# Smaller steps, earlier loads, another order of the second sweep, and the sums of w1 on VectorE, in a fused retention and mixture-of-experts kernel

## The chip, the cores and the metric

The kernel runs on one core of one Trainium2 chip. The metric is device time in microseconds (us), taken as the median of several executions. Engines are named as the profile names them: PE is TensorE (PEld its weight loads), DVE is VectorE, ACT is ScalarE, POOL is GpSimd, SP is SyncE, which here only issues DMAs.

## The reference

```python
def _attn_ref(q, k, v):                       # B, H, S, D = 4, 8, 768, 64
    gamma = 1.0 - 2.0 ** (-5.0 - np.arange(H))
    for t in range(S):
        state = gamma[None, :, None, None] * state + einsum('bhd,bhe->bhde', k[:, :, t], v[:, :, t])
        y[:, :, t] = einsum('bhd,bhde->bhe', q[:, :, t], state) / sqrt(D)

def _moe_ref(x, w_gate, w1, w2):              # N, D, E, F = 3072, 512, 8, 1024
    logits = x @ w_gate
    P = np.exp(logits - logits.max())
    for _ in range(8):
        P /= P.sum(1, keepdims=True) + 1e-09
        P /= P.sum(0, keepdims=True) + 1e-09
        P *= N / E
    for e in range(E):
        out += P[:, e:e + 1] * (np.maximum(x @ w1[e], 0.0) @ w2[e])
```

The output of the first function, laid out as 3072 tokens by 512, is the x of the second.

## The kernel before

The program has three stages, and within each engine the instructions run in the order in which the code is written: no scheduler moves them, and every queue, SP's DMA queue too, is served in order.

**Attention.** The retention is computed in 24 chunks of 128 steps (6 chunks for each of 4 batch entries). The loop variable is `tau`. One pass loads the four raw tiles of chunk tau + 3 (`loads`), splits q and k of chunk tau + 2 into a rounded part and a remainder (`split_qk`: `kh`, `QH` on ACT, `QL` on DVE, `kl` on POOL), computes the scores of chunk tau + 1 (`ps_s`, then `ta` on DVE), the gate logits of chunk tau - 1, and the result of chunk tau (`attend`: `ps_x`, `RX`), which SP stores to `xd`; `state` updates the running state with `tk` and `st` from POOL. Four chunks make a position c of the sequence. After pass `tau == 2 * B` (8) the loop also works off a list `todo`, two tasks a pass, which prepares the next stage.

**First product** (x @ w1, relu). It is a Strassen-like scheme: each 2x2 block product is made with seven products M1 to M7 of sums of blocks. For x these sums and their split into rounded part (hi, ACT) and remainder (lo) are made by `x_tasks`, from tiles that `x_load` fetches from `xd`; XSC holds the sums for a while. There are three groups r of two sequence positions; X0 holds r = 0 and later r = 2, X1 holds r = 1. For w1 one job is one 512 KB load into one half of RW (`w1_load`), four sums of 128x256 (`adds`), the rounding of the 7 blocks and two remainders (3 and 4 blocks) into one of three buffers WA (`w1_tasks`).

`UnitA` is one output block: seven products of 6 matmuls of 128x512, each followed by work on its PSUM bank. A row of the main loop (variable n, 96 rows) walks through `ROW`, seven places m = 0 to 6: M6 of unit n, M1 of unit n + 1, M3, M7, M2 of n + 1, M5 of n + 1, M4. The DVE work of a row is, by the profile's lines, L213 and L214 (after M3), L218 (after M7), L225 (after M2), L234 and L236 (`sums`, m = 4) and L240 (`last_sum`, m = 0 of the next row). Four PSUM banks are shared: M5 reuses M3's bank, M4 reuses M7's, so PE can go on only when DVE has read them.

The first 32 rows (the first sweep) run r = 0 with a new w1 job in each row; a job is prepared in the row two ahead of its use, from the queue `wq` at places m = 0, 1 and 5. The queue `xq` prepares X1 in rows 0 to 10 and, from row 32 on, the tile X0 for r = 2. Then the second sweep runs r = 1 and r = 2: units 29, 30, 31 with r = 1, the same three with r = 2, and then each unit with both. `order` is the list that says which job, unit and r a row has. A list `sink` holds the Sinkhorn steps (max, exp, eight times `sink_a` and `sink_b`, a transpose), one per row from row 12 on; each uses DVE and small matmuls at the end of a row.

**Second product** (h @ w2, weighted sum): the third stage reads the stored h back; the change doesn't touch its code.

Of the kernel before, what the change touches and what calls it, by code (L numbers as in the profile page):

```python
# [47 lines left out]
def kernel(  # L48
# [60 lines left out]
    def x_load(t, r):  # L109
        for i, c, d in ((M1, 0, 0), (M7, 1, 0), (M3, 1, 1), (M2, 0, 1)):  # L110
            for k in range(2):
                sp.dma_start(rd(t[:, XP[i], 1, k * 512:(k + 1) * 512]).rearrange("p (b s) -> p b s", s=C),  # L112
                             xd[2 * r + c][:, :, 2 * d + k, :])

    def x_tasks(t, engs):
        q = []
        sc = {M7: 0, M5: 1, M6: 2, M4: 3}
        e = [engs[k % len(engs)] for k in range(22)]
        for k in range(2):
# [6 lines left out]
            def tt(o, a, b, src=src):  # L126
                eng = e.pop()
                q.append(lambda: eng.tensor_tensor(XSC[:, sc[o], :], a, b, ALU.subtract))

            def one(i, w=w, src=src):  # L130
                eng = e.pop()

                def f():
                    hi_act(w(i, 0), src(i))
                    lo(eng, w(i, 1), src(i), w(i, 0))
                q.append(f)

            b12 = rd(w(M7))
            tt(M5, b12, src(M1))
            tt(M6, src(M3), src(M5))  # L140
            tt(M7, src(M3), b12)
            tt(M4, src(M2), src(M6))
            for i in (M1, M5, M2, M6, M7, M3, M4):
                one(i)
# [677 lines left out]
```

## Time and profile before

| what | value |
|---|---|
| median of 3 runs | 2055.17 us (2054.22 to 2057.34) |
| the profiled execution, its own time | 2053.89 us |
| its span | 2051.8 us |
| mean granted TensorE clock | 0.987 |
| busy PE / DVE / ACT / POOL | 1985.9 / 1527.7 / 1041.7 / 406.0 us |
| HBM read and written | 269.31 and 232.88 MB |
| first matmul of the first product | at 166.28 us |
| first row of the second sweep, loads of X0 issued | at 501.27 us |

A line of a timeline gives start, duration, engine, line of the code, operation, tile written and tiles read, shape, count of instructions merged, and in brackets how long the engine stood idle before and what it waited for. A line of a table by stretches gives, for each engine, its busy time and the number of instructions begun; PEclk is the granted clock as a share of full speed.

### The profile page before, as it was taken

The numbers are of one execution on the slowest core, as the hardware profiler recorded it, in microseconds if no ns is written. First come the engines' busy times: TensorE is split into PE (matmuls) and PEld (weight loads), VectorE is DVE, ScalarE is ACT, GpSimd is POOL, SyncE is SP. The second block draws the span as 40 slices with busy tenths as digits, with TensorE's granted clock in tenths as the row PEclk, the third lists the DMA queues.
The fourth block names the chain that finished last, engine by engine and source line by source line (L and its number), as shares of the span: only waits on it lengthen the run. The fifth ranks groups of instructions, "written<-read, shape, count | busy, mean of one in ns | idle before, by whom it ended". The sixth has DMA issues, their size and how long they took to land.

```text
span 2051.8 us, 28824 instructions
## 1 busy us (share of the span) xinstructions
PE 1985.9 (97%) x9273; PEld 1647.2 (80%) x9273; DVE 1527.7 (74%) x2083; ACT 1041.7 (51%) x1668; POOL 406.0 (20%) x422
## 2 busy tenths in 40 slices
PE   7797999998899999999999999999999999999998
PEld 7786887887688888888887788888888888888887
DVE  6795988995666666666677787878778777868766
ACT  3343564554444444444444565655555555655553
POOL 5462342341211121121123000100100101001001
PEclk9899999999999999999999999999999999999999
DMA  7755776776466666666667888998999999999997
GB/s 240 239 180 163 242 245 206 244 244 217 165 233 214 218 228 217 221 218 223 220 229 263 297 286 281 278 288 277 285 283 278 267 291 270 291 292 269 271 269 184
DMA packets 253191, 504.13 MB, mean 246 GB/s; under 512 B 27824, under 2 KB 40432, under 8 KB 250992
## 3 DMA queue, kind: packets, MB, share of 16 engines
q1 hardware_dynamic: 241088, 458.78, 66.3%
q0 software_dynamic: 11952, 43.52, 11.0%
q8 instruction: 72, 1.18, 0.2%
q14 instruction: 79, 0.65, 0.1%
HBM read 269.31 MB, written 232.88 MB: 245 GB/s over the span
## 4 chain that ended last, share of the span: by engine, by line
PE 90%; DVE 4%; DMA 3%; issue 1%; ACT 1%; SPq 1%; POOL 0%; DVEq 0%; ACTq 0%
PE psA L190 42%; PE psA L551 25%; PE psB L551 19%; DMA raw<-kT 1%; DVE QL L80 1%; PE ps_s L327 1%; PE ps_x L363 1%; DMA RW<-w 1%; PE psA L372 1%; PE ps_x L358 0%; PE ps_t L339 0%; DVE X L80 0%; DVE ta L330 0%; SPq L112 0%; DMA hd<-OT 0%
## 5 line engine op out<-in xcount | busy, mean ns | idle before, releaser
L190 PE MATMUL psA<-X,WA 128*128 128x512 f32 x4032 | 931.4, 393 | 24.1 <-DVE OT L213 18.8
L190 PEld LDWEIGHTS psA<-X,WA 128*128 128x128 f32 x4032 | 760.8, 189 | 190.2 <-DVE OT L213 20.9
L77 ACT ACTIVATE WA<-WA 128x512 fp32r<-128x512 f32 x668 | 403.1, 629 | 259.3 <-PE psB L551 116.7
L551 PE MATMUL psA<-WA,X 128*128 128x512 f32 x2296 | 531.4, 389 | 0.2 <-DVE XSC L562 0.2
L551 PEld LDWEIGHTS psA<-WA,X 128*128 128x128 f32 x2296 | 431.0, 188 | 89.9 <-issue 0.6
L551 PE MATMUL psB<-WA,X 128*128 128x512 f32 x1728 | 404.3, 390 | 5.1 <-ACT WA L77 3.1
L80 DVE TENSOR_TENSOR WA<-WA,WA 128x512 fp32r<-128x512 f32 x487 | 313.7, 685 | 99.4 <-ACT WA L77 94.9
L551 PEld LDWEIGHTS psB<-WA,X 128*128 128x128 f32 x1728 | 324.6, 188 | 74.8 <-ACT WA L77 4.2
L158 POOL TENSOR_TENSOR RW<-RW 128x256 f32<-128x256 f32 x244 | 220.8, 915 | 637.9 <-DMA RW<-w 412.8
L219 ACT ACTIVATE OT<-OT 128x512 f32<-128x512 f32 x96 | 60.7, 632 | 243.3 <-DVE OT L218 243.3
L80 DVE TENSOR_TENSOR WA<-RW,WA 128x768 fp32r<-128x768 f32 x122 | 142.5, 1169 | 54.0 <-ACT WA L77 53.9
L569 POOL DMA_DIRECT2D out<-XSC x56 | 48.5, 865 | 611.7 <-DVE XSC L564 365.6
L80 DVE TENSOR_TENSOR WA<-WA 128x512 fp32r<-128x512 f32 x181 | 121.7, 697 | 35.4 <-ACT WA L77 34.4
L213 DVE TENSOR_TENSOR OT<-psA,OT 128x512 f32<-128x512 f32 x96 | 66.2, 689 | 106.2 <-PE psA L190 106.2
L77 ACT ACTIVATE WA<-RW 128x768 fp32r<-128x768 f32 x122 | 109.4, 946 | 23.6 <-POOL RW L158 13.9
L225 DVE TENSOR_TENSOR OT<-psA,OT 128x512 f32<-128x512 f32 x96 | 66.2, 690 | 58.5 <-ACT OT L219 51.3
L229 ACT ACTIVATE OT<-psA 128x512 f32<-128x512 f32 x96 | 57.5, 599 | 77.1 <-PE psA L190 40.3
L236 DVE TENSOR_TENSOR OT<-OT 128x512 f32<-128x512 f32 x96 | 92.2, 961 | 3.3
L579 ACT ACTIVATE OT<-psA 128x512 f32<-128x512 f32 x96 | 57.4, 598 | 72.7 <-PE psA L551 68.8
L226 ACT ACTIVATE OT<-OT 128x512 f32<-128x512 f32 x96 | 60.7, 633 | 65.4 <-DVE OT L225 65.3
L240 DVE TENSOR_TENSOR OT<-OT 128x512 f32<-128x512 f32 x96 | 70.1, 730 | 30.0 <-ACT OT L229 26.1
L211 ACT ACTIVATE OT<-psA 128x512 f32<-128x512 f32 x96 | 57.4, 598 | 64.0 <-PE psA L190 63.9
(116 smaller groups left out, 1486.4 us busy)
## 6 DMA issues: line engine op xcount, KB each, us to landing
hd<-OT SPq DMA_DIRECT2D x672, 256.0 KB, 2.6
WA<-hd SPq DMA_DIRECT2D x668, 256.0 KB, 6.1
RW<-w SPq DMA_DIRECT2D x61, 512.0 KB, 4.5
out<-XSC POOLq DMA_DIRECT2D x56, 512.0 KB, 8.3
RW<-w SPq DMA_DIRECT2D x16, 1024.0 KB, 7.7
out<-OT POOLq DMA_DIRECT2D x27, 512.0 KB, 8.4
OT<-pd SPq DMA_DIRECT2D x23, 512.0 KB, 6.2
raw<-kT SPq DMA_DIRECT2D x24, 256.0 KB, 4.0
```

The source lines that it names most:

```text
L77: act.activation(o, i, AF.Copy)
L80: eng.tensor_tensor(o, full, rd(h), ALU.subtract)
L158: eng_add.tensor_tensor(x[:, WP[o]], x[:, WP[p]], x[:, WP[q]], op)
L190: pe.matmul(ps, w[:, a, k * P:(k + 1) * P], x[:, b, k * 512:(k + 1) * 512], start=i in PRE and k == 0 and m == 0, stop=k == 1 and m == 2, ...
L213: dve.tensor_tensor(c12, ps, u2, ALU.add)
L219: act.activation(o, o, AF.Relu)
L225: dve.tensor_tensor(o, ps, s1, ALU.add)
L226: act.activation(o, o, AF.Relu)
L229: act.activation(self.new("A12"), ps, AF.Relu)
L236: dve.tensor_tensor(t["S2"], t["S1"], t["A11"], ALU.subtract)
L240: dve.tensor_tensor(self.new("S4"), self.t["A12"], self.t["S2"], ALU.subtract)
L551: pe.matmul(ps[d] if isinstance(ps, tuple) else ps[:, d, :], w[:, a, q * 256 + d * P:q * 256 + d * P + P], h[b], start=i in PRE and q == 0 ...
```

## The change

It has six parts.

- The loads of X0 for r = 0 are split: the first position after pass 5, the second after pass 8, there behind the two w1 loads. The task list then starts with the two w1 jobs (POOL sums, now in a step of their own; the rounding is a second step), followed by the x tasks; it is run from pass 10 on. Two more w1 loads are issued after pass 16 instead of at the first rows.
- `x_tasks` becomes 22 equal steps: one subtraction (always DVE) or one remainder, and at most one rounding on ACT for a later step.
- In the rows, `w1_tasks` has four steps at m = 0, 3, 5 and 6, and its sums run on DVE instead of POOL.
- X1 is prepared from row 1 on, two steps a row; X0 for r = 2 from row 33 on, five steps a row, two remainders in seven on POOL.
- The second sweep runs units 29 to 31 with r = 1, units 28, 27, 26 with r = 1 and then r = 2, units 29 to 31 with r = 2 (their w1 is loaded and prepared a second time, so there are 64 jobs instead of 61), and then as before.
- The max becomes three sink steps and the exp three of six operations; the list starts at row 14, and the transpose comes at row 38.

```diff
-    def x_load(t, r):
-        for i, c, d in ((M1, 0, 0), (M7, 1, 0), (M3, 1, 1), (M2, 0, 1)):
-            for k in range(2):
+    def x_load(t, r, which=(0, 1)):
+        for i, c, d in ((M1, 0, 0), (M2, 0, 1), (M7, 1, 0), (M3, 1, 1)):
+            for k in range(2) if c in which else ():
...
+            def step(n, w=w, src=src):
+                b12 = rd(w(M7))
+                hi = [M1, M2, M5, M6, M7, M3, M4][n] if n < 7 else None
+                if n < 4:
+                    o, a, b = [(M5, b12, src(M1)), (M6, src(M3), src(M5)), (M7, src(M3), b12), (M4, src(M2), src(M6))][n]
+                    dve.tensor_tensor(XSC[:, sc[o], :], a, b, ALU.subtract)
+                else:
+                    i = [M1, M5, M2, M6, M7, M3, M4][n - 4]
+                    lo(engs[n % len(engs)], w(i, 1), src(i), w(i, 0))
+                if hi is not None:
+                    hi_act(w(hi, 0), src(hi))
...
+        def rounded():
             hi_act(a[:, 0:3, 0, :], x[:, 0:3, :])
             hi_act(a[:, 3:7, 0, :], x[:, 3:7, :])
...
-        return [adds, lambda: rest(slice(0, 3)), lambda: rest(slice(3, 7))]
+        return [adds, rounded, lambda: rest(slice(0, 3)), lambda: rest(slice(3, 7))]
...
-    for g in [[NJ - 3, NJ - 2, NJ - 1]] + [[j] for j in range(NJ - 4, 2, -1)] + [[2, 1, 0]]:
-        order += [(j if j >= NJ - 3 else 2 * NJ - 4 - j, j, r) for r in (1, 2) for j in g]
+    order += [(j, j, 1) for j in (NJ - 3, NJ - 2, NJ - 1)]
+    order += [(NJ + k, NJ - 4 - k, r) for r in (1, 2) for k in range(3)]
+    order += [(NJ + 3 + k, NJ - 3 + k, 2) for k in range(3)]
+    for g in [[j] for j in range(NJ - 7, 2, -1)] + [[2, 1, 0]]:
+        order += [(2 * NJ - 1 - j, j, r) for r in (1, 2) for j in g]
...
+                if tau == B + 1:
+                    x_load(X0, 0, (0,))
                 if tau == 2 * B:
-                    x_load(X0, 0)
                     w1_load(0)
                     w1_load(1)
-                    todo += x_tasks(X0, [dve]) + w1_tasks(0, pool, dve) + w1_tasks(1, pool, dve)
-                if tau > 2 * B:
+                    todo += [f for g in zip(w1_tasks(0, pool, dve), w1_tasks(1, pool, dve)) for f in g]
+                    x_load(X0, 0, (1,))
+                    todo += x_tasks(X0, [dve])
+                if tau > 2 * B + 1:
                     run(todo, 2)
+                if tau == 4 * B:
+                    w1_load(2)
+                    w1_load(3)
...
-        sink = [sink_max, sink_exp] + [sink_a, sink_b] * SINKHORN + [sink_t]
+        sop = sink_exp()
+        sink = [sink_max, sink_max2, sink_max3]
+        sink += [lambda k=k: run(sop, 6) for k in range(3)]
+        sink += [sink_a, sink_b] * SINKHORN + [sink_t]
...
-                wq += w1_tasks(conv, pool, dve)
+                wq += w1_tasks(conv, dve, dve)
...
-                xq = x_tasks(X0, [dve, pool])
+            if n == NJ + 1:
+                xq = x_tasks(X0, [dve, dve, pool])
...
-                if m in (0, 1, 5):
+                if m in (0, 3, 5, 6):
                     run(wq, 1)
-                if m in (1, 6) or n >= NJ:
-                    run(xq, 2 if n >= NJ else 1)
+                if m in (1, 6) or n >= NJ and m in (0, 3, 5):
+                    run(xq, 1)
```

How this stands on the engines is shown at three places. First DVE, in a row of the first sweep in which X1 is prepared: of the row's names, X is X1, OT holds temporary and output blocks, psA the PSUM banks. Before:

```order
L80 TENSOR_TENSOR WA_72<-RW,WA_72 128x3x256
L80 TENSOR_TENSOR X_1773<-XSC,X_1773 128x512
L213 TENSOR_TENSOR OT<-psA_256,OT 128x512
L214 SCALAR_TENSOR_TENSOR OT<-OT 128x512
L218 TENSOR_TENSOR OT<-psA_253,OT 128x512
L225 TENSOR_TENSOR OT<-psA_255,OT 128x512
L234 SCALAR_TENSOR_TENSOR OT<-OT 128x512
L236 TENSOR_TENSOR OT<-OT 128x512
L80 TENSOR_TENSOR WA_72<-RW,WA_72 128x4x256
L80 TENSOR_TENSOR X_1773<-X_1773 128x512
L240 TENSOR_TENSOR OT<-OT 128x512
```

And now, on the same engine, in such a row:

```order
L152 TENSOR_TENSOR RW<-RW 128x256 x4
L80 TENSOR_TENSOR X_1775<-X_1775 128x512
L209 TENSOR_TENSOR OT<-psA_256,OT 128x512
L210 SCALAR_TENSOR_TENSOR OT<-OT 128x512
L214 TENSOR_TENSOR OT<-psA_253,OT 128x512
L221 TENSOR_TENSOR OT<-psA_255,OT 128x512
L230 SCALAR_TENSOR_TENSOR OT<-OT 128x512
L232 TENSOR_TENSOR OT<-OT 128x512
L80 TENSOR_TENSOR WA_71<-RW,WA_71 128x3x256
L80 TENSOR_TENSOR WA_71<-RW,WA_71 128x4x256
L80 TENSOR_TENSOR X_1775<-XSC,X_1775 128x512
L236 TENSOR_TENSOR OT<-OT 128x512
```

The four sums stand ahead of the reads of PSUM (now L209 to L221), and both remainders of w1 stand together behind the row's sums.

Second, DVE in row 35, the third row of the second sweep in which X0 is prepared for r = 2 (L131 and L80 on X_70), with w1 job 34:

```order
L152 TENSOR_TENSOR RW<-RW 128x256 x4
L80 TENSOR_TENSOR X_70<-XSC,X_70 128x512
L131 TENSOR_TENSOR XSC<-X_70 128x512
L209 TENSOR_TENSOR OT<-psA_256,OT 128x512
L210 SCALAR_TENSOR_TENSOR OT<-OT 128x512
L214 TENSOR_TENSOR OT<-psA_254,OT 128x512
L131 TENSOR_TENSOR XSC<-X_70,XSC 128x512
L221 TENSOR_TENSOR OT<-psA_255,OT 128x512
L230 SCALAR_TENSOR_TENSOR OT<-OT 128x512
L232 TENSOR_TENSOR OT<-OT 128x512
L80 TENSOR_TENSOR WA_72<-RW,WA_72 128x3x256
L131 TENSOR_TENSOR XSC<-X_70 128x512
```

Before, the same preparation stood in rows 32 and 33, fourteen tasks a row, with every second operation on POOL.

Third, SP around pass 8 of the attention, where the raw tiles of chunk 12 (raw0 to raw3) are loaded. Before:

```order
L368 DMA xd2_77<-RX_280 128x512
L112 DMA X0_70<-xd0_75 128x4x128 x2
L112 DMA X0_70<-xd1_76 128x4x128 x4
L112 DMA X0_70<-xd0_75 128x4x128 x2
L152 DMA RW_73<-w1 128x1024 x2
L284 DMA raw0_887<-qT 128x512
L284 DMA raw1_889<-kT 128x512
```

And now:

```order
L367 DMA xd2_77<-RX_280 128x512
L146 DMA RW_73<-w1 128x1024 x2
L112 DMA X0_70<-xd1_76 128x4x128 x4
L283 DMA raw0_887<-qT 128x512
L283 DMA raw1_889<-kT 128x512
```

Four of the eight loads of X0 left this place; they stand in the same way ahead of the raw tiles of chunk 9.

More of the change, by code (lines that the diff above doesn't have):

```diff
@@ L124, in src @@
                 return XSC[:, sc[i], :] if i in sc else rd(w(i))
[L126 to L144, printed above, removed]
+            def step(n, w=w, src=src):
[9 more added lines that the diff above has]
+                    hi_act(w(hi, 0), src(hi))
+            q += [lambda n=n, step=step: step(n) for n in range(11)]
         return q
@@ L459, in sink_exp @@
             dve.tensor_copy(mx, ps[:, 0:1])
+        def sink_exp():
             x, n, r, q = [et[:, i, :] for i in range(4)]
             s1, s2 = [ei[:, i, :].bitcast(mybir.dt.int32) for i in range(2)]
-            l2 = L.rearrange("p a b -> p (a b)")
-            dve.tensor_scalar(x, l2, mx, -104.0, ALU.subtract, ALU.max)
-            dve.tensor_scalar(n, x, LOG2E, MAGIC, ALU.mult, ALU.add)
-            dve.tensor_scalar(n, n, MAGIC, None, ALU.subtract)
-            dve.scalar_tensor_tensor(r, n, -LN2_HI, x, ALU.mult, ALU.add)
@@ L467, in sink_exp @@
-            dve.scalar_tensor_tensor(r, n, -LN2_LO, r, ALU.mult, ALU.add)
-            dve.tensor_scalar(x, n, -126.0, None, ALU.max)
-            dve.tensor_tensor(n, n, x, ALU.subtract)
-            dve.tensor_scalar(s1, x, 127.0, 8388608.0, ALU.add, ALU.mult)
-            dve.tensor_scalar(s2, n, 127.0, 8388608.0, ALU.add, ALU.mult)
-            dve.tensor_scalar(q, r, EXPC[0], None, ALU.mult)
-            for c in EXPC[1:]:
-                dve.scalar_tensor_tensor(q, q, c, r, ALU.add, ALU.mult)
@@ L475, in sink_exp @@
-            p2 = Pm.rearrange("p a b -> p (a b)")
-            dve.scalar_tensor_tensor(q, q, 1.0, s1.bitcast(F32), ALU.add, ALU.mult)
-            dve.tensor_tensor(p2, q, s2.bitcast(F32), ALU.mult)
+            l2, p2 = [t.rearrange("p a b -> p (a b)") for t in (L, Pm)]
+            ops = [
+                lambda: dve.tensor_scalar(x, l2, mx, -104.0, ALU.subtract, ALU.max),
+                lambda: dve.tensor_scalar(n, x, LOG2E, MAGIC, ALU.mult, ALU.add),
+                lambda: dve.tensor_scalar(n, n, MAGIC, None, ALU.subtract),
+                lambda: dve.scalar_tensor_tensor(r, n, -LN2_HI, x, ALU.mult, ALU.add),
+                lambda: dve.scalar_tensor_tensor(r, n, -LN2_LO, r, ALU.mult, ALU.add),
+                lambda: dve.tensor_scalar(x, n, -126.0, None, ALU.max),
+                lambda: dve.tensor_tensor(n, n, x, ALU.subtract),
+                lambda: dve.tensor_scalar(s1, x, 127.0, 8388608.0, ALU.add, ALU.mult),
+                lambda: dve.tensor_scalar(s2, n, 127.0, 8388608.0, ALU.add, ALU.mult),
+                lambda: dve.tensor_scalar(q, r, EXPC[0], None, ALU.mult),
+            ]
@@ L479, in sink_a @@
+            ops += [lambda c=c: dve.scalar_tensor_tensor(q, q, c, r, ALU.add, ALU.mult) for c in EXPC[1:]]
+            ops += [
+                lambda: dve.scalar_tensor_tensor(q, q, 1.0, s1.bitcast(F32), ALU.add, ALU.mult),
+                lambda: dve.tensor_tensor(p2, q, s2.bitcast(F32), ALU.mult),
+            ]
+            return ops
         def sink_a():
@@ L714 @@
             UA[0].post(i)
-        loaded = 3
+        loaded = 4
         PS2 = None
@@ L760 @@
                 loaded += 1
-            if 12 <= n < 12 + len(sink):
-                sink[n - 12]()
+            if 14 <= n < 13 + len(sink):
+                sink[n - 14]()
+            if n == 38:
+                sink[-1]()
         carry.last_sum()
```

10 lines of the change are left out of this document (5 added, 5 removed).

## The prediction

> **What bounds the kernel now.** I read the page's busy times first, then the chain of work that ended last, then TensorE's matmuls by stretches, and last the timelines at the places where the stretches lose time. The busy times and one piece of the chain (start, length, what):
>
> ```profile
> PE 1985.9 (97%) x9273; PEld 1647.2 (80%) x9273; DVE 1527.7 (74%) x2083; ACT 1041.7 (51%) x1668; POOL 406.0 (20%) x422
> 537.53 571.94 PE psA L190 x2520
> 505.25 5.66 DMA X<-xd
> 171.86 6.85 DMA RW<-w
> ```
>
> TensorE bounds it. In the undisturbed piece a matmul takes 571.94 / 2520 = 0.227 us, so a row of the first product (42 matmuls) takes 9.53 us, and nothing of the change makes a matmul shorter: it can only win or lose time in which TensorE waits. The matmuls of line L190 alone, by stretches (length, PE busy and count, PEld, granted clock, DMA share, GB/s), show where it does:
>
> ```profile
> 166.20:202.20 36.00, 28.06 (x108) 22.10 (x108) 0.91 0.61 188
> 202.20:307.70 105.50, 105.01 (x457) 84.93 (x456) 1.00 0.74 244
> 307.70:341.00 33.30, 27.96 (x108) 22.19 (x109) 0.90 0.61 192
> 341.00:500.00 159.00, 159.00 (x692) 128.89 (x691) 1.00 0.70 233
> 500.00:540.00 40.00, 27.56 (x102) 20.68 (x101) 0.87 0.53 170
> 540.00:1109.00 569.00, 569.00 (x2510) 470.50 (x2509) 1.00 0.64 221
> ```
>
> Length minus count times 0.227 is the loss: 11.5 us at the start, 1.8 in the rows that prepare X1, 8.8 at the max and the exp, 1.9 in the Sinkhorn rows (mostly the small matmuls, which stay), 16.8 where X0 is prepared for r = 2, none after. That is 40.8 us, all that can be won here. The rest, attention, ends at 166 us.
>
> **The start, 11.5 us.** The chain shows w1 job 2 landing late: its load is issued at 171.86, behind the loads of X1, and takes 6.85 us; job 3 follows in the same way. The change issues both after pass 16, more than 30 us earlier, and X1's steps begin one row later. I leave 1.0: gain 10.5.
>
> **The rows with the sums on DVE.** This is the part that can turn against it, since every row's PSUM reads stand behind the sums on an engine that is nearly full. One row of DVE while POOL was idle, the remainder of three blocks, and the prices near a sum of 128x256:
>
> ```profile
> 182.23 0.68 DVE L213 TENSOR_TENSOR OT<-psA,OT 128x512 f32<-128x512 f32 x1
> ...
> 184.50 0.69 DVE L225 TENSOR_TENSOR OT<-psA,OT 128x512 f32<-128x512 f32 x1 [0.26 <-ACT OT L207]
> ...
> 186.43 1.22 DVE L80 TENSOR_TENSOR WA<-RW,WA 128x1024 fp32r<-128x1024 f32 x1
> 187.57 0.68 DVE L128 TENSOR_TENSOR XSC<-X,XSC 128x512 f32<-128x512 f32 x1
> 188.17 0.69 DVE L240 TENSOR_TENSOR OT<-OT 128x512 f32<-128x512 f32 x1
> ...
> 397.60 0.95 DVE L80 TENSOR_TENSOR WA<-RW,WA 128x768 fp32r<-128x768 f32 x1
> 398.47 0.68 DVE L213 TENSOR_TENSOR OT<-psA,OT 128x512 f32<-128x512 f32 x1
> L661 DVE TENSOR_TENSOR RW<-RW 128x512 f32<-128x512 f32 x56 | 38.3, 684 | 0.0
> L483 DVE TENSOR_TENSOR Pm<-Pm,rs 128x192 f32<-128x192 f32 x7 | 2.5, 358 | 0.2
> L158 POOL TENSOR_TENSOR RW<-RW 128x256 f32<-128x256 f32 x244 | 220.8, 915 | 637.9 <-DMA RW<-w 412.8
> L80 DVE TENSOR_TENSOR WA<-RW,WA 128x1024 fp32r<-128x1024 f32 x61 | 82.7, 1357 | 0.0
> L236 DVE TENSOR_TENSOR OT<-OT 128x512 f32<-128x512 f32 x96 | 92.2, 961 | 3.3
> ```
>
> From start to start: L213 to L225 less its wait 2.01, L225 to the remainder of four blocks 1.93, that remainder 1.14, L240 as long as the step at L128, 0.60, the remainder of three blocks 0.87: 6.55 us. A sum isn't in the trace; its bounds are 0.36 (128x192) and 0.68 (128x512), and between them by the count of elements 0.42, nearest to the smaller one. Four of them make 1.7, the row 8.25, against 9.53 of TensorE. Two steps of X1 add 1.2: 9.45, just under. So rows 1 to 11 cost nothing, as long as POOL leaves DVE alone, and it does: the same remainder that took 1.22 alone has a mean of 1.36, and L236 one of 0.96 against 0.69, because POOL's sums run beside them, and these are gone. I leave 1.5 of the 1.8 lost now: gain 0.3.
>
> **The sink.** Its rows, and the stall that the exp makes:
>
> ```profile
> 323.16 1.93 DVE L474 SCALAR_TENSOR_TENSOR XSC<-XSC 128x192 f32<-128x192 f32 x5
> 329.98 15.38 PE L190 MATMUL psA<-X,WA 128*128 128x512 f32 x54 [2.88 <-DVE OT L213]
> 385.68 0.15 DVE L489 TENSOR_SCALAR ct<-pcs 128x8 f32<-128x8 f32 x1
> 386.38 0.68 DVE L240 TENSOR_TENSOR OT<-OT 128x512 f32<-128x512 f32 x1
> 395.24 0.34 DVE L480 TENSOR_REDUCE rs<-Pm 128x24 f32<-128x192 f32 x1
> 397.00 0.68 DVE L240 TENSOR_TENSOR OT<-OT 128x512 f32<-128x512 f32 x1
> ```
>
> `sink_a` takes 1.76 and `sink_b` 0.70. With the sums a row with `sink_a` needs 10.0 (0.5 over), the next 8.95 (0.6 under); DVE may lag some 1.5 us before TensorE stands, since M5 needs M3's bank only two products later, but what it makes good in the second row it can only make good while it lags. Between nothing and 0.5 for each of the 7 `sink_a` before row 33: I take 2.0. Three rows with six operations of the exp at 0.39 or less need up to 10.6: 2.0. The small matmuls stay, 1.9. So 5.9 instead of 10.7, and the transpose no longer waits for a max in its own row: gain 4.8.
>
> **The second sweep.** The stall of 16.8 us begins with the loads of X0 for r = 2 (in the chain above), which can't start before row 31 is done, and the fourteen tasks a row behind them. Now r = 2 is wanted in row 37, five rows later, so the loads are covered by rows 32 to 34, and 22 steps are spread over rows 33 to 37. What is late next is DVE: rows 33, 34 and 35 each carry a w1 job (8.25), three to five steps at 0.60 on DVE, and a sink step: 11.95, 11.8 and 11.95. That is 7.1 over, less the 1.5 of lag: 5.6 (nothing to 10). Jobs 29 to 31 done again add 3 x 3.7 on DVE in rows 39 to 41, which have 8.25 and no other work, and 1.5 MB of loads at a DMA share of 0.64: hidden. Gain 11.2.
>
> **Attention, about nothing.** The eight loads of X0 and two of w1 after pass 8 hold up the raw tiles of chunk 12 and all behind (SP, ACT, PE, and two stretches of all engines: PE, PEld, DVE, ACT, POOL, clock):
>
> ```profile
> 63.70 6.97 SPq L112 DMA_DIRECT2D X<-xd  x8
> 72.44 0.65 SPq L284 DMA_DIRECT2D raw<-kT  x1
> 79.54 0.63 ACT L77 ACTIVATE kh<-raw 128x512 fp32r<-128x512 f32 x1 [14.61 <-DMA raw<-kT]
> 84.37 0.55 PE L327 MATMUL ps_s<-QH,kh 128*128 128x256 f32 x1 [10.28 <-DVE ta L330]
> 78.00:84.00 6.00, 0.00 (x0) 0.00 (x0) 3.22 (x3) 2.92 (x5) 3.75 (x3) 0.50 0.85 325
> 84.00:90.00 6.00, 5.63 (x26) 5.66 (x27) 5.89 (x11) 1.78 (x3) 1.65 (x2) 0.50 0.60 179
> 149.03 1.06 ACT L77 ACTIVATE WA<-RW 128x1024 fp32r<-128x1024 f32 x1 [3.46 <-POOL RW L158]
> ```
>
> TensorE stands 10.3 us and then runs a while at half its clock, some 4 us more. Four of the loads (3.5 us of issue) now stand in front of chunk 9 instead: a stall there of about 3.5, and one of about 5.5 after pass 8, with the half clock behind at least the second, 4. That is 13 to 17 against 14.3. The eight POOL sums (8 x 0.915 = 7.3 us) now stand in one block after pass 10, ahead of `tk`, `kl` and `st` of the next pass; TensorE waits for the raw tiles just then, which hides them; without that cover they cost up to 7. In exchange ACT no longer stands 3.46 us behind POOL near the end, and the remainders no longer wait for their rounding. The two w1 loads after pass 16 cost about 1. I take 0, between -8 and +10.
>
> [...]
>
> **Sum.** 10.5 + 0.3 + 4.8 + 11.2 + 0 = 26.8 us. The profiled execution took 2053.89 (its span 2051.8 and 2.1 around it), 1.3 under the median of the runs. 2053.9 - 26.8 = 2027; by the median 2028. I say 2029, for small waits of the first rows that I haven't priced.
>
> **Rivals.**
>
> (a) DVE can't carry the rows; slower. If a sum costs 0.80, midway between DVE's row of 512 and POOL's 0.915 for the same sum, a row is 9.75: over by 1.4 in the 11 rows with X1, by 1.45 on average in the 13 rows of `sink_a` and `sink_b`, by 2.5 in the three of the exp, by 0.2 in the 5 others, and rows 33 to 35 lose 4.6 more: 47.5 us, where the sum above has 5.5. That is 42 more, 2071. For it speaks that all of PSUM's sums wait on this one engine; against it the 0.36 for 192 elements. It ends above the kernel before from 0.72 a sum on; at 0.5 it gives 2035. 7 in 100.
>
> (b) The sums wait for their load on DVE. POOL waited for it 412.8 us in all, at no cost; DVE would stand with every PSUM read behind it. A half of RW is free only when the remainder at the end of row n is done, and the sums come at the start of row n + 2, nearly 10 us later, against some 5 for issue and landing. If 0.5 us a row is lost on 30 rows: 2044. 9 in 100.
>
> (c) Attention pays: both stalls run into the half clock and POOL's block isn't covered: 10 more, 2039. 17 in 100.
>
> (d) Attention gains: the split loads mostly hide in the slack, and the shorter tail counts: 8 less, 2021. 16 in 100.
>
> **How the numbers follow.** The forecast, 2029 with its own range of 2024 to 2035, has 50 in 100. The range takes in (d) and (b) with what lies around them and leaves out (a) at the top: 2018 to 2047. Within 0.2% (2051 to 2059, about what a measurement of this kernel can tell from no change) lie only mixtures, several terms at their bad ends, 9 in 100; slower is (a), 7; faster 84.
>
> **What would show it.** Right: L190 begins near 166 us; the stretches at the start and at the exp lose under 2 and under 4 us; POOL has nothing between attention and the end of the first product but four steps on X0; the sums at L152 take 0.40 to 0.45, and TensorE's waits lie in rows 33 to 36. It would be wrong if matmuls wait for L209 in most rows of the first sweep (a), if L152 waits for RW (b), or if L190 begins over 8 us from 166 (c, d).

## The result and the profile after

| kernel | median (us) | runs | ratio to the kernel before, 95% interval |
|---|---|---|---|
| before | 2055.16 (2054.22 to 2057.34) | 4 | |
| changed | 2034.4 (2030.9 to 2036.94) | 4 | 0.9896 [0.9881, 0.9912] |
| changed, run again | 2033.05 (2027.32 to 2036.51) | 6 | 0.9904 [0.9886, 0.9922] |

The change makes the kernel 1.0% faster. The time lies in the range (2018 to 2047), 5 us above the predicted 2029. The profiled execution took 2033.8 us, its span 2031.9. Its busy times, and the group of the moved sums (busy time, mean ns of one, idle before):

```profile
PE 1983.3 (98%) x9273; PEld 1646.8 (81%) x9273; DVE 1560.1 (77%) x2344; ACT 1038.4 (51%) x1674; POOL 181.6 (9%) x179
L152 DVE TENSOR_TENSOR RW<-RW 128x256 f32<-128x256 f32 x248 | 99.5, 422 | 4.3
```

TensorE's busy time is what it was; POOL's fell from 406.0 to 181.6 us and DVE's rose by 32. A sum takes 0.422 us on DVE. The matmuls of the first product (now line L186), by stretches as in the prediction (length, PE busy and count, PEld, clock, DMA share, GB/s):

```profile
171.30:274.00 102.70, 102.63 (x444) 84.03 (x444) 0.98 0.74 236
274.00:340.20 66.20, 65.93 (x290) 53.98 (x289) 1.00 0.78 250
340.20:390.00 49.80, 49.23 (x212) 39.53 (x213) 1.00 0.74 238
390.00:487.60 97.60, 97.47 (x420) 77.76 (x419) 1.00 0.70 229
487.60:563.80 76.20, 69.22 (x295) 54.62 (x296) 1.00 0.70 225
563.80:1088.00 524.20, 524.20 (x2314) 433.98 (x2314) 1.00 0.66 223
```

The stalls at the start and at the exp are gone: TensorE is busy for nearly all of the first four stretches. It still stands 7 us where X0 is prepared for r = 2. And the first matmul comes 5.1 us later than before, at 171.37.

For a finer view, row n of the first product is taken to begin with its matmul number 18 + 42 n, and its loss is its length less 9.53 us. These sums over rows come from the traces:

| profiled execution | first matmul at | rows 0 to 11 | 12 to 31 | 32 to 39 | 40 to 91 | all rows |
|---|---|---|---|---|---|---|
| before | 166.28 | 13.1 | 11.4 | 17.2 | -0.2 | 41.6 |
| changed | 171.37 | 0.5 | 5.0 | 9.5 | -0.5 | 14.4 |
| changed, run again | 172.09 | 0.4 | 4.9 | 9.1 | -0.5 | 13.9 |

So the rows won 27.2 us. Of this, 6.6 is lost again before row 0 begins (170.50 before, 177.13 after: 5.1 in the attention and 1.5 in the first 18 matmuls, which run partly at half clock, 0.50 from 171.24 to 174.65; in the second run of the changed kernel the clock is 1.00 from 168 to 174, and row 0 begins at 176.31), and 0.7 behind the rows (0.3 in the second run). That makes 19.9, the difference of the two spans.

The rows of one kernel repeat from run to run within some tenths of a us; the attention doesn't. That is why small differences below are read from rows, and the medians only to some 3 us.

### The profile page after: what moved, and what is told of

The parts are those of the page before. It is cut to its first block, busy times and chain, and to the rows that moved or that the text cites. A ratio compares the mean times of both kernels' runs of the same rounds, so it can differ in the third digit from the quotient of the medians.

```text
span 2031.9 us, 28760 instructions
## 1 busy us (share of the span) xinstructions
PE 1983.3 (98%) x9273; PEld 1646.8 (81%) x9273; DVE 1560.1 (77%) x2344; ACT 1038.4 (51%) x1674; POOL 181.6 (9%) x179
## 4 chain that ended last, share of the span: by engine, by line
PE 90%; DVE 4%; DMA 2%; issue 1%; ACT 1%; SPq 1%; POOL 1%; DVEq 0%; ACTq 0%; POOLq 0%
PE psA L186 43%; PE psA L566 26%; PE psB L566 19%; DMA raw<-kT 1%; DVE QL L80 1%; PE ps_s L326 1%; PE ps_x L362 1%; PE ps_x L357 0%; PE psA L371 0%; DMA WA<-hd 0%; DVE ta L329 0%; DMA hd<-OT 0%; PE ps_t L338 0%; DVE X L80 0%; DMA gq<-c_gq 0%
## 5 line engine op out<-in xcount | busy, mean ns | idle before, releaser
L186 PE MATMUL psA<-X,WA 128*128 128x512 f32 x4032 | 925.0, 391 | 8.2 <-ACT OT L225 4.2
L186 PEld LDWEIGHTS psA<-X,WA 128*128 128x128 f32 x4032 | 756.3, 188 | 172.3 <-ACT OT L225 10.3
L80 DVE TENSOR_TENSOR WA<-WA,WA 128x512 fp32r<-128x512 f32 x487 | 314.0, 686 | 99.3 <-ACT WA L77 94.8
L80 DVE TENSOR_TENSOR WA<-WA 128x512 fp32r<-128x512 f32 x181 | 121.7, 697 | 36.5 <-ACT WA L77 32.7
L209 DVE TENSOR_TENSOR OT<-psA,OT 128x512 f32<-128x512 f32 x96 | 66.2, 689 | 108.7 <-PE psA L186 108.7
L80 DVE TENSOR_TENSOR WA<-RW,WA 128x768 fp32r<-128x768 f32 (+1 forms) x128 | 134.9, 1094 | 0.1
L77 ACT ACTIVATE WA<-RW 128x768 fp32r<-128x768 f32 (+1 forms) x128 | 114.0, 938 | 3.0 <-POOL RW L152 2.9
L221 DVE TENSOR_TENSOR OT<-psA,OT 128x512 f32<-128x512 f32 x96 | 66.2, 690 | 56.7 <-ACT OT L215 48.8
L152 DVE TENSOR_TENSOR RW<-RW 128x256 f32<-128x256 f32 x248 | 99.5, 422 | 4.3
L236 DVE TENSOR_TENSOR OT<-OT 128x512 f32<-128x512 f32 x96 | 67.0, 698 | 34.6 <-ACT OT L225 34.5
L232 DVE TENSOR_TENSOR OT<-OT 128x512 f32<-128x512 f32 x96 | 68.4, 712 | 3.3
```

Source lines behind the costliest of these rows:

```text
L77: act.activation(o, i, AF.Copy)
L80: eng.tensor_tensor(o, full, rd(h), ALU.subtract)
L152: eng_add.tensor_tensor(x[:, WP[o]], x[:, WP[p]], x[:, WP[q]], op)
L186: pe.matmul(ps, w[:, a, k * P:(k + 1) * P], x[:, b, k * 512:(k + 1) * 512], start=i in PRE and k == 0 and m == 0, stop=k == 1 and m == 2, ...
L209: dve.tensor_tensor(c12, ps, u2, ALU.add)
L221: dve.tensor_tensor(o, ps, s1, ALU.add)
```

## The experiments

Each is the changed kernel with one edit, unless the text says otherwise. They ran in three groups, with the kernel before at 2054.18, 2052.22 and 2053.86 us (11 runs each); the changed kernel ran again in the second (2033.05).

| kernel | median (us) | ratio [95%] | first matmul | rows 0 to 11 | 12 to 31 | 32 to 39 | all rows |
|---|---|---|---|---|---|---|---|
| sums on POOL | 2042.82 | 0.995 [0.9933, 0.9967] | 174.69 | 3.4 | 6.3 | 9.2 | 18.9 |
| sums doubled | 2081.89 | 1.0144 [1.0128, 1.0159] | 173.36 | 17.7 | 29.0 | 13.5 | 63.3 |
| old start | 2041.95 | 0.9939 [0.992, 0.9957] | 172.99 | 9.1 | 5.0 | 9.4 | 22.9 |
| old sink | 2038.86 | 0.9931 [0.9914, 0.9947] | 168.83 | 0.5 | 11.2 | 6.6 | 17.7 |
| old second sweep | 2043.14 | 0.9949 [0.9934, 0.9964] | 177.21 | 0.6 | 5.0 | 16.6 | 21.6 |
| old attention | 2028.42 | 0.9873 [0.9856, 0.989] | 170.60 | 0.1 | 5.0 | 9.4 | 14.0 |
| w1 loads late | 2031.91 | 0.9903 [0.9888, 0.9918] | 169.05 | 0.4 | 4.9 | 9.6 | 14.4 |
| spread loads | 2027.53 | 0.987 [0.9855, 0.9885] | 165.91 | 0.2 | 4.9 | 9.4 | 14.0 |
| deep raw tiles | 2011.98 | 0.9803 [0.9787, 0.9818] | 150.24 | 0.4 | 4.9 | 9.4 | 14.2 |
| before, deep raw tiles | 2042.78 | 0.9942 [0.9925, 0.996] | 156.48 | 11.4 | 13.3 | 17.5 | 41.8 |
| all that helped | 2012.61 | 0.9799 [0.9781, 0.9817] | 156.22 | 0.1 | 5.6 | 6.5 | 11.7 |

### The sums of w1: back on POOL, and doubled on DVE

```diff
-                wq += w1_tasks(conv, dve, dve)
+                wq += w1_tasks(conv, pool, dve)
```

> The changed kernel with one part undone: in the rows the sums of w1 run on POOL again. Theory (a DVE budget per row): DVE loses 1.7 us of sums a row but its ops with two SBUF inputs grow again beside POOL (the remainder of four blocks from 1.2 to about 1.6, the sums of the outputs by 0.2 to 0.4 each), so a row falls from 8.25 to some 7.3 to 7.7 us, under TensorE's 9.53 in either case. Plain rows and rows with X1 stay as they are; the Sinkhorn rows and rows 33 to 35, which are over, lose 1 to 4 us less: 2030 to 2034 against 2034.4 of the changed kernel. Rival (taking the sums off POOL, and with it POOL's slowing of DVE, is where the gain of the first product comes from): 2042 or more.

Measured: 2042.82 us, 9.8 above the changed kernel's second run; its rows lose 4.5 us more, 2.9 of it in rows 0 to 11 and 1.3 in rows 12 to 31, and its first matmul came 2.6 to 3.3 us later, though nothing of the attention is edited. So some 4.5 of the difference is shown to come from the sums, and the rival is nearer than the theory. The reason is seen in the busy times and DVE's groups, first with the sums on POOL:

```profile
PE 1989.8 (98%) x9273; PEld 1647.5 (81%) x9273; DVE 1545.9 (76%) x2096; ACT 1039.4 (51%) x1674; POOL 431.9 (21%) x427
...
L232 DVE TENSOR_TENSOR OT<-OT 128x512 f32<-128x512 f32 x96 | 92.0, 958 | 3.3
L80 DVE TENSOR_TENSOR WA<-RW,WA 128x1024 fp32r<-128x1024 f32 x64 | 91.8, 1436 | 0.0
L152 POOL TENSOR_TENSOR RW<-RW 128x256 f32<-128x256 f32 x256 | 256.8, 1013 | 627.4 <-DMA RW<-w 471.1 <-DVE OT L214 101.4 <-DVE OT L210 33.2
```

and then in the changed kernel:

```profile
L232 DVE TENSOR_TENSOR OT<-OT 128x512 f32<-128x512 f32 x96 | 68.4, 712 | 3.3
L80 DVE TENSOR_TENSOR WA<-RW,WA 128x1024 fp32r<-128x1024 f32 x64 | 79.0, 1235 | 0.0
```

The two groups alone take 36.4 us more of DVE time with the sums on POOL. In all, DVE is busy 1545.9 us there and 1560.1 with 99.5 us of sums on it: taking them off DVE saves it only 14 us, since the other 85 come back as instructions that last longer while POOL (1.013 us a sum) is at work. That is why the move costs no row anything.

The doubled sums are eight instructions instead of four, which write the same values again:

```diff
-            tt(M5, M7, M4, ALU.add)
-            tt(M6, M5, M1, ALU.subtract)
-            tt(M3, M2, M6, ALU.subtract)
+            for o in range(3 if eng_add is dve else 1):
+                tt(M5, M7, M4, ALU.add)
+            for o in range(2 if eng_add is dve else 1):
+                tt(M6, M5, M1, ALU.subtract)
+            for o in range(2 if eng_add is dve else 1):
+                tt(M3, M2, M6, ALU.subtract)
```

> The changed kernel with the sums of w1 in the rows done twice (eight operations instead of four, the same result). Theory (a row costs what DVE's starts add up to, 8.25 us, beside TensorE's 9.53, and nothing is lost until they pass it): plus 1.7 a row makes plain rows 9.95, rows with X1 11.15, with sink_a 11.7 and sink_b 10.65: about 18 us in rows 1 to 11, 9 in 14 to 19, 20 in 20 to 31, 15 in 32 to 39, nothing after 42, where only every second row has a job; in all 45 to 55 us more than the changed kernel, 2079 to 2090. Rival (it is the place of the sums ahead of the PSUM reads that costs, with every row hit alike, also after row 42): 0.5 us or more a row there. Second rival (DVE has idle time that takes them): under 15 us more.

Measured: 2081.89, 48.8 above the changed kernel, and 49.4 in the rows. Rows 2 to 11 lose 1.75 on average, and of rows 44 to 91, whose DVE has nothing but its row and the sums, only two lose over 0.3. This is the theory's place and size. One sum still takes the same time:

```profile
L152 DVE TENSOR_TENSOR RW<-RW 128x256 f32<-128x256 f32 x496 | 205.0, 424 | 12.8
```

### The start: w1 jobs 2 and 3 loaded at the first rows again

```diff
-                if tau == 4 * B:
-                    w1_load(2)
-                    w1_load(3)
...
         wq, xq = [], []
+        w1_load(2)
...
-        loaded = 4
+        loaded = 3
```

> The changed kernel with one part undone: w1 jobs 2 and 3 are loaded at the first rows again, behind the eight loads of X1, and not after pass 16. Theory (the start's gain comes from these two loads alone): rows 0 to 3 lose 9 to 13 us more than the 0.5 that the changed kernel loses there, the matmuls of the other rows start as before, and the time is 2041 to 2046, some 8 to 12 above the changed kernel (2033). Rival (the start's gain came mostly from X1's steps beginning a row later): rows 0 to 3 lose under 4, and the time is under 2038.

Measured: 2041.95, 8.9 above; rows 0 to 3 lose 9.0 (1.4, 7.3, 0.3, 0.0). DVE's timeline, and TensorE's, show what the theory named:

```profile
198.31 1.68 DVE L152 TENSOR_TENSOR RW<-RW 128x256 f32<-128x256 f32 x4 [5.42 <-DMA RW<-w]
```

```profile
201.25 13.95 PE L186 MATMUL psA<-X,WA 128*128 128x512 f32 x48 [3.46 <-DVE OT L209]
```

DVE stands 5.42 us for the load of job 3, whose sums stand in front of L209, and TensorE waits 3.46 us for that; then 48 matmuls take 13.95 us instead of 10.9, since the granted clock is 0.70 and 0.73 in the 12 us from 198 on. The rest of what the first rows lost before (13.1 in rows 0 to 11) is left for X1's steps, which begin a row later, and for the other edits there; that part wasn't undone by itself.

### The sink in its old steps

```diff
-        sink = [sink_max, sink_max2, sink_max3]
-        sink += [lambda k=k: run(sop, 6) for k in range(3)]
+        sink = [lambda: (sink_max(), sink_max2()), lambda: (sink_max3(), run(sop, 18))]
...
-            if 14 <= n < 13 + len(sink):
-                sink[n - 14]()
-            if n == 38:
-                sink[-1]()
+            if 12 <= n < 12 + len(sink):
+                sink[n - 12]()
```

> The changed kernel with one part undone: the max is one step with its transpose, the exp one step of 18 operations, the list starts at row 12 and ends with the transpose at row 30. Theory 1 (DVE's work counts in both places): rows 12 to 15 lose 6 to 9 us more, rows 33 to 36 win back 2 to 3 of the 9 that they lose, since three sink steps (3.2 us of DVE) leave them; 2036 to 2040. Theory 2 (rows 33 to 36 wait for the late store of an output block, not for DVE's work): the same loss in rows 12 to 15 and nothing won back; 2039 to 2043. Rival: the single step hides behind TensorE's queue, and the time is within 2 us of the changed kernel (2033).

Measured: 2038.86. Rows 12 to 15 lose 6.7 more (2.0, 0.5, 3.0, 1.2), rows 34 and 35 win back 2.2 (3.7 and 1.0 instead of 4.1 and 2.8). Theory 1 holds. TensorE stands at the max and behind the exp:

```profile
299.38 0.27 PE L460 MATMUL pmx<-ident,mx 128*1 128x128 f32 x1 [1.80 <-DVE mx L456]
...
319.05 4.39 PE L186 MATMUL psA<-X,WA 128*128 128x512 f32 x18 [2.49 <-DVE OT L209]
```

### The second sweep in its old order

```diff
-    order += [(j, j, 1) for j in (NJ - 3, NJ - 2, NJ - 1)]
-    order += [(NJ + k, NJ - 4 - k, r) for r in (1, 2) for k in range(3)]
-    order += [(NJ + 3 + k, NJ - 3 + k, 2) for k in range(3)]
-    for g in [[j] for j in range(NJ - 7, 2, -1)] + [[2, 1, 0]]:
-        order += [(2 * NJ - 1 - j, j, r) for r in (1, 2) for j in g]
+    for g in [[NJ - 3, NJ - 2, NJ - 1]] + [[j] for j in range(NJ - 4, 2, -1)] + [[2, 1, 0]]:
+        order += [(j if j >= NJ - 3 else 2 * NJ - 4 - j, j, r) for r in (1, 2) for j in g]
...
-            if n == NJ + 1:
                 xq = x_tasks(X0, [dve, dve, pool])
...
-                if m in (1, 6) or n >= NJ and m in (0, 3, 5):
-                    run(xq, 1)
+                if m in (1, 6) or n >= NJ:
+                    run(xq, 2 if n >= NJ else 1)
```

> The changed kernel with the order of the second sweep undone: units 29 to 31 with r = 1, then with r = 2, and X0 for r = 2 prepared in rows 32 and 33, two of the small steps at each place. Theory (the loads of X0 and the 22 steps stand in front of row 34's M1): the stretch from row 32 to the first undisturbed row loses 15 to 19 us as in the kernel before, instead of 9.2: 2040 to 2046. Rival (what mattered there was the size of the steps and POOL's share in them, the order is indifferent): within 2 us of the changed kernel, 2032 to 2037.

Measured: 2043.14, within the expected times; rows 32 to 39 lose 16.6 instead of 9.5, in two long waits:

```profile
507.00 12.26 PE L186 MATMUL psA<-X,WA 128*128 128x512 f32 x42 [6.42 <-DVE OT L209]
522.02 4.59 PE L186 MATMUL psA<-X,WA 128*128 128x512 f32 x12 [2.76 <-DVE OT L209]
```

The new order is worth 7.1 us. The steps of `x_tasks` stayed small here, so that part, with the sums on DVE, wins next to nothing in the second sweep without the new order (the kernel before loses 17.2).

### The attention in its old order

All of the change's edits in the loop over `tau` are undone, and the two w1 loads stand behind the list:

```diff
-                if tau == B + 1:
-                    x_load(X0, 0, (0,))
                 if tau == 2 * B:
+                    x_load(X0, 0)
                     w1_load(0)
                     w1_load(1)
-                    todo += [f for g in zip(w1_tasks(0, pool, dve), w1_tasks(1, pool, dve)) for f in g]
-                    x_load(X0, 0, (1,))
-                    todo += x_tasks(X0, [dve])
-                if tau > 2 * B + 1:
+                    todo += x_tasks(X0, [dve]) + w1_tasks(0, pool, dve) + w1_tasks(1, pool, dve)
+                if tau > 2 * B:
                     run(todo, 2)
-                if tau == 4 * B:
-                    w1_load(2)
-                    w1_load(3)
...
             run(todo, 20)
+            w1_load(2)
+            w1_load(3)
```

> The changed kernel with the attention part undone: all eight loads of X0 and the two w1 loads after pass 8, the x tasks ahead of the w1 tasks from pass 9 on, and w1 jobs 2 and 3 loaded only when the list is done, right ahead of X1's loads. Theory (the split burst made two stalls out of one, and TensorE's half clock is paid after each): the first matmul of the first product comes near 167 us instead of 171.4, and 0 to 3 us are lost at the first rows by the later w1 loads: 2029 to 2033. Rival (attention's 5 us come from the eight POOL sums in one block, or from the w1 loads of jobs 2 and 3): then this one still has the POOL sums near the end, ACT waits for them there, and it stays at 2033 to 2036.

Measured: 2028.42, some 5 us below the changed kernel, with the same rows. So this part of the change costs about 5 us by the medians, as the theory says. The first matmul isn't near 167 in the profiled execution (170.60), which is the slowest of the four. The intervals of the ratios touch (0.9856 to 0.989, and 0.9886 to 0.9922).

### Where the attention's 5 us went: three edits of the loads

First only the two w1 loads after pass 16, moved behind the list:

```diff
-                if tau == 4 * B:
-                    w1_load(2)
-                    w1_load(3)
...
             run(todo, 20)
+            w1_load(2)
+            w1_load(3)
```

> The changed kernel with the loads of w1 jobs 2 and 3 taken from pass 16 and issued when the list is done, right ahead of X1's loads. Theory (these two loads delay the raw tiles of a pass, TensorE stands about 3 us at 138 and runs at half clock to 150): 3 to 7 us less than the changed kernel in the same call, with at most 1 us lost in the first rows. Rival (DVE is behind there and hides it): within 2 us of it.

Measured: 2031.91, 1.1 below the changed kernel, inside both intervals. The half clock near 144 us (0.50 from 143.93 to 150.76 in the changed kernel) does go with these two loads: with the raw tiles three passes ahead, the clock falls between 138 and 151 us in the changed kernel's two runs, sums on POOL, old second sweep and old sink, which have both loads after pass 16, and stays at 1.00 there in the three that have neither (this one, old start, old attention). But the time hardly moves, so they explain little of the 5 us.

Then X0's loads one at a time behind passes 5 to 12, the w1 loads after passes 2, 4, 14 and 16, and the POOL sums in single steps:

```diff
...
+            pieces = {5: ((M1,), (0,)), 6: ((M2,), (0,)), 7: ((M1,), (1,)), 8: ((M7,), (0,)),
+                      9: ((M3,), (0,)), 10: ((M2,), (1,)), 11: ((M7,), (1,)), 12: ((M3,), (1,))}
...
-                if tau == B + 1:
-                    x_load(X0, 0, (0,))
+                if tau in pieces:
+                    x_load(X0, 0, *pieces[tau])
...
```

> The changed kernel with the attention's loads spread: one 256 KB load of X0 after each of passes 5 to 12, the w1 loads one each after passes 2, 4, 14 and 16, the w1 tasks in passes 6 to 10 (no more than one POOL block of four sums in a pass), the x tasks from pass 11 on. Theory (the 5 us lost in attention, and the 14 us lost there before, are raw tiles that wait behind bursts of loads, with TensorE's half clock after each stall): no stall over 3 us, first matmul of the first product at 152 to 158 us: 2014 to 2022. Rival (behind the stalls attention is bound by DVE, whose work is the same, and by POOL): at most 4 us earlier, 2030 or more.

Measured: 2027.53, between the two expectations: some 6 us won, but the clock still falls to half three times (from 62.8, 83.3 and 114.0 us).

Last, the raw tiles loaded four passes ahead instead of three, with one buffer more for each kind:

```diff
-            nbuf = [4, 4, 4, 3]
+            nbuf = [5, 5, 5, 4]
...
                 if tau == 2:
                     loads(4)
+                    loads(5)
...
-                loads(tau + 3)
+                loads(tau + 4)
```

> The changed kernel with the raw tiles loaded four passes ahead instead of three, with one more buffer each. Theory (attention loses its time where raw tiles, which land only about 1 us before they are needed, wait behind the bursts of loads): the stalls after passes 5, 8 and 16 and the half clock behind them go, attention is then bound by DVE, first matmul of the first product at 152 to 160 us, 2015 to 2024. Rival (the bursts fill the DMA queues themselves, so earlier issue only moves the wait; POOL's block and ACT's waits do the rest): first matmul at 166 us or later, 2028 or more.

Measured: 2011.98, more than was expected: 21 us below the changed kernel, all of it ahead of the first matmul (150.24 instead of 171.4 to 172.1). What ACT's `kh` waited for from 20 to 172 us (total, times, longest), in the changed kernel:

```profile
ACT kh L77 <- DMA raw<-kT: 75.9, 18, 11.7
```

and with the deep raw tiles:

```profile
ACT kh L77 <- DMA raw<-kT: 31.2, 5, 9.7
```

So not only the places where loads were moved, but most passes of the attention had waited for raw tiles that came a little late.

### The same edit on the kernel before

> The kernel before with one thing added: the raw tiles are loaded four passes ahead instead of three (one buffer more for each of the four kinds). Theory (in both kernels attention loses its time to raw tiles that come late behind the loads of X0 and w1, and nothing else of attention changed): the first matmul of the first product comes at 148 to 154, as in the changed kernel with the same edit (150.2), the rows lose the same 41 to 42 us, and the time is 2035 to 2043. Rival (the kernel before gains less, since its eight loads in one place are still too many): first matmul at 156 to 164, 2044 to 2051.

Measured: 2042.78, 11 below the kernel before; first matmul at 156.48, where the rival has it, and the time where the theory has it: both are met by half. ACT now waits mostly for TensorE, and for raw tiles three times only; but one of these waits is as long as before, 14.5 us after pass 8, behind the ten loads in one place:

```profile
ACT kh L77 <- PE ps_s L327: 41.8, 13, 5.1
ACT kh L77 <- DMA raw<-kT: 22.6, 3, 14.5
```

With raw tiles three passes ahead the change's attention begins the first product 5 us later than the old one; with four passes that loss is gone. How much is gained instead is less sure: the two profiled executions are 6 us apart (156.48 and 150.24), but the one of the kernel before is the slowest of its six and the other the fastest of its four. The medians are 30.8 us apart, the ratios 28.5 us, and the rows take 27.6 of it, so some 1 to 3 us are left, no more than the medians can resolve.

### All that helped, together

The deep raw tiles, the spread loads, the sink from row 11 on (over at row 32), and the loads of X0 for r = 2 in four pairs behind the products of row 32:

```diff
...
+                if n == NJ and m < 4:
+                    x_load(X0, 2, (M1, M7) if m % 2 == 0 else (M3, M2), (m // 2,))
...
-            if 14 <= n < 13 + len(sink):
-                sink[n - 14]()
+            if 11 <= n < 10 + len(sink):
+                sink[n - 11]()
...
```

> The changed kernel with everything that helped: raw tiles four passes ahead, the loads of X0 and w1 in attention spread over passes 2 to 16, the sink's list from row 11 on (so that it is over at row 32), and the loads of X0 for r = 2 in four pairs behind the products M6, M1, M3 and M7 of row 32 instead of all ahead of it. Theory: first matmul at 144 to 151, rows 33 to 36 lose 3 to 6 us instead of 9, 2002 to 2009. Rival (those rows are bound by the w1 sums and X0's steps on DVE alone): they lose 8 to 9 as before, and the time is 2009 to 2014.

Measured: 2012.61, no better than the deep raw tiles alone: the rows are at the theory's upper end, the time is in the rival's range. The rows won 2.5 us (11.7 instead of 14.2), and row 35 lost 1.0 instead of 2.8, which is the 1.76 us of the `sink_a` that left row 34. But the spread loads, which helped the short prefetch, don't help the long one: the first product begins 6 us later in the profiled executions (156.22 against 150.24), and 2 to 3 us later by the medians less the rows. Rows 34 to 36 still lose 6.0; the next section shows with what. Both of these versions beat the kernel before by 2.0%.

## Why the prediction was right, and where it was wrong

| term | predicted gain | in the rows | by undoing it |
|---|---|---|---|
| start, and X1's rows | 10.5 + 0.3 | 12.6 | 8.6 (the loads alone) |
| sink | 4.8 | 6.4 | 3.3 (6.2 less 2.9 won back) |
| second sweep | 11.2 | 7.7 | 7.1 |
| rows together | 26.8 | 27.2 | |
| attention up to row 0 | 0 | -6.6 | about -5 |
| behind the rows | not named | -0.7 | |

**The price of a sum** decided the sign, and it was right: 0.42 taken, 0.422 measured, and rows 1 to 11 lose 0.5 in all. Rival (a) is shown to be real as a mechanism: with the sums doubled, 0.85 us for each two, the kernel is slower than before (1.0144 [1.0128, 1.0159]). Its own price for 0.80 was 42 us over the forecast; at 0.85 the rows gave 49.4.

**The sums waiting for their load**, rival (b), didn't come: the group at L152 stood idle 4.3 us in all 248 sums, with no DMA named. The old start shows that it can (5.42 us for one late load).

**The start and the sink** came out somewhat better than predicted, with the mechanism right: the first 12 rows lose 0.5 where 2.5 was left, rows 12 to 31 lose 5.0 where 5.9 was left, and the loss before in those rows was 11.4 rather than the 10.7 that the stretches gave.

**The second sweep** is the term in the rows that was mis-sized: 5.6 left was predicted, 9.5 is lost. DVE's timeline in the first two rows with X0's steps:

```profile
506.02 0.69 DVE L221 TENSOR_TENSOR OT<-psA,OT 128x512 f32<-128x512 f32 x1 [1.53 <-DMA hd<-OT]
506.63 0.68 DVE L230 SCALAR_TENSOR_TENSOR OT<-OT 128x512 f32<-128x512 f32 x1
507.35 1.67 DVE L232 TENSOR_TENSOR OT<-OT 128x512 f32<-128x512 f32 x1
...
510.41 2.31 DVE L80 TENSOR_TENSOR WA<-RW,WA 128x1024 fp32r<-128x1024 f32 x1
```

and POOL's, SP's and TensorE's around them:

```profile
506.84 1.63 POOL L80 TENSOR_TENSOR X<-XSC,X 128x512 fp32r<-128x512 f32 x1 [349.16 <-PE psA L186]
510.29 1.35 POOL L80 TENSOR_TENSOR X<-XSC,X 128x512 fp32r<-128x512 f32 x1 [1.83 <-DMA hd<-OT]
```

```profile
489.06 6.80 SPq L112 DMA_DIRECT2D X<-xd  x8
495.96 4.48 SPq L196 DMA_DIRECT2D hd<-OT  x7
```

```profile
509.75 5.71 PE L186 MATMUL psA<-X,WA 128*128 128x512 f32 x24 [1.33 <-ACT OT L225]
517.48 4.41 PE L186 MATMUL psA<-X,WA 128*128 128x512 f32 x18 [2.02 <-DVE OT L209]
...
529.69 3.03 PE L186 MATMUL psA<-X,WA 128*128 128x512 f32 x12 [1.31 <-DVE OT L209]
```

Two things are missing in the prediction's sum. DVE stood 1.53 us at L221, time that the sum had counted as usable. The profile names an output block whose store was issued behind the eight loads of X0 (they hold SP from 489.06 to 495.86); but in the last kernel, shown below, the store is in time and DVE stands 1.48 us at the same place, for TensorE's product. So the late store adds little to that wait. And the two steps on POOL, priced at nothing, slow what DVE does beside them: L232 takes 1.67 where its mean in this kernel is 0.71, and the remainder of four blocks 2.31 where the prediction's row has 1.22. That is 2.1 us more in two rows. The 5.6 predicted, 1.5 and 2.1 make 9.2, against 9.5 measured. The prediction had used the slowing of DVE beside POOL for the first sweep, and left it out here. The remainder begins 0.12 us after POOL's step (510.41 and 510.29) and ends 1.08 us after it (512.72 and 511.64); the prediction's row has 1.22 for the whole of it.

In the last kernel the store is in time and the sink over, and the two instructions beside POOL's first steps are as slow as here:

```profile
489.38 0.69 DVE L221 TENSOR_TENSOR OT<-psA,OT 128x512 f32<-128x512 f32 x1 [1.48 <-PE psA L186]
...
490.71 1.67 DVE L232 TENSOR_TENSOR OT<-OT 128x512 f32<-128x512 f32 x1
...
493.76 2.31 DVE L80 TENSOR_TENSOR WA<-RW,WA 128x1024 fp32r<-128x1024 f32 x1
```

Without the three sink steps (3.2) the prediction's 5.6 would be 2.4; with 1.5 and 2.1 that makes 6.0, which is what rows 34 to 36 lose there. A step of X0 takes DVE 0.60 us, and on POOL it takes DVE 0.96 and 1.09 (1.67 less 0.71, 2.31 less 1.22). That putting all of X0's steps on DVE would win the difference was not run.

The gains of the three terms are off by +1.8, +1.6 and -3.5 us; that these cancel is why the sum of the rows came out right to 0.4.

**The attention** makes up the whole of the 5 us between 2029 and the measured time. The price was taken as 0 between -8 and +10, with rival (c) at +10. What failed is the step "13 to 17 against 14.3": it counted two stalls, with the half clock behind at least the second. In fact the clock falls four times between 50 and 165 us (all engines, then the clock, DMA share and GB/s):

```profile
60.00:66.00 6.00, 3.68 (x20) 3.71 (x21) 5.83 (x9) 1.78 (x3) 3.59 (x3) 0.72 0.38 131
...
84.00:90.00 6.00, 3.46 (x17) 3.49 (x17) 5.86 (x9) 4.01 (x6) 5.76 (x7) 0.50 0.27 91
90.00:96.00 6.00, 6.00 (x35) 5.45 (x36) 2.24 (x4) 3.12 (x5) 5.92 (x7) 0.50 0.44 144
...
114.00:120.00 6.00, 4.38 (x25) 4.41 (x26) 5.86 (x10) 2.82 (x5) 1.60 (x2) 0.72 0.43 134
120.00:126.00 6.00, 6.00 (x46) 5.45 (x46) 3.73 (x8) 1.78 (x3) 3.27 (x3) 0.71 0.54 173
...
144.00:150.00 6.00, 6.00 (x36) 5.45 (x36) 4.53 (x8) 0.99 (x2) 1.32 (x2) 0.50 0.54 175
```

and in the kernel before twice, once at pass 8 and once here:

```profile
132.00:138.00 6.00, 6.00 (x36) 5.45 (x35) 4.29 (x8) 1.88 (x4) 2.24 (x3) 0.50 0.62 178
```

Ahead of each of the four TensorE stands still. The first is the stall at pass 5, which the prediction put at about 3.5 us: TensorE stood 3.29 us, and then a matmul of the scores took 0.41 us (0.28 at full clock). The other three follow below it:

```profile
62.32 0.55 PE L326 MATMUL ps_s<-QH,kh 128*128 128x256 f32 x1 [3.29 <-DVE ta L329]
62.67 0.41 PE L326 MATMUL ps_s<-QL,kh 128*128 128x256 f32 x1
...
86.54 0.55 PE L326 MATMUL ps_s<-QH,kh 128*128 128x256 f32 x1 [6.64 <-DVE ta L329]
...
115.62 0.36 PE L326 MATMUL ps_s<-QH,kh 128*128 128x256 f32 x1 [2.42 <-ACT QH L77]
...
142.57 0.36 PE L326 MATMUL ps_s<-QH,kh 128*128 128x256 f32 x1 [2.38 <-DVE ta L329]
```

The first two were foreseen, and the second shrank from 10.28 to 6.64 us where 5.5 was expected; but half clock came with both (0.50 from 62.01 to 65.43 and from 82.49 to 96.15). The last two were not foreseen; the kernel before has one such stall, of 1.92 us. In all TensorE stood 14.7 us in these places and the half clock lasted 30.7 us, against 12.2 and 23.9 in the kernel before. ACT stood for a raw tile ahead of the first two:

```profile
57.48 0.63 ACT L77 ACTIVATE kh<-raw 128x512 fp32r<-128x512 f32 x1 [7.04 <-DMA raw<-kT]
...
81.71 0.63 ACT L77 ACTIVATE kh<-raw 128x512 fp32r<-128x512 f32 x1 [11.74 <-DMA raw<-kT]
```

and ahead of the last two as well (4.79 us up to 113.78, 6.60 up to 137.72). The raw tiles were late without the moved loads too; the same waits from 20 to 172 us in the kernel before:

```profile
ACT kh L77 <- DMA raw<-kT: 72.3, 16, 14.6
```

That is nearly the 75.9 of the changed kernel. The gain that was set against the second stall isn't seen as long as raw tiles are late; with the deep raw tiles the loss of 5 us is gone. The drop near 144 goes with the two w1 loads after pass 16, which the prediction priced at 1. Why TensorE stood 2.42 us near 115, with half clock behind it, stays open.

What was to show the prediction right came as written, but for the first: L190's successor begins 5.4 us from 166 (the bound was 8); the start and the exp lose less than 2 and 4; POOL stands idle for 349 us ahead of its first step on X0; and TensorE's waits lie in rows 34 to 36.

## What to carry to other kernels

Before loads are moved within a stage, ask how early that stage's own tiles arrive: one pass more of prefetch was worth 21 us on the changed kernel, as much as all six parts of the change together, and 11 on the kernel before, and with it the moved loads no longer cost their 5 us. A step that is given to an idle engine isn't free when it holds up the engine that bounds the row: price it by what a neighbour's instruction takes beside it (1.67 us against 0.71), not by its own time. A wait that the profile puts down to a transfer isn't won by an earlier transfer alone: without the late store DVE stood as long for TensorE (1.48 us against 1.53). And a sum that comes out right has to be read term by term, since here errors of 2 to 4 us cancelled.
